# Half of one token group's first layer as seven products of halves, in an attention + squared-ReLU kernel on one core

## The chip, the core and the metric

One of the eight cores of a Trainium2 chip runs the whole kernel. The metric is the time of one execution on the device, in microseconds (us). The engines named below are PE (TensorE, the matrix multiplier; PEld is its weight load), DVE (VectorE), ACT (ScalarE), POOL (GpSimd) and SP (SyncE, which here only issues DMAs).

## What is computed

```
scores = q @ k^T / 8 + bias            # 8 batches, 8 heads, 576 tokens, head size 64
x      = softmax(scores) @ v           # heads put side by side: x is 4608 x 512
h      = max(x @ w_in, 0)              # layer 1: w_in is 512 x 2048
out    = (h * h) @ w_out               # layer 2: w_out is 2048 x 512, out is 4608 x 512
```

Inputs and output are float32. Inside, matrices are float16 and sums float32.

## The kernel before

**Two parts.** Attention goes over 32 pairs of heads (`pair(p)`, four for each batch). The two layers go over NG = 9 groups of GT = 512 tokens (`layers(g)`, L1084). A batch has 576 tokens, so group 7 (tokens 3584 to 4095) and group 8 (4096 to 4607) both need rows of the last batch, and their layer 1 comes after the last pair.

**Attention of a pair.** PE makes scores into the two tiles `st` of PSUM (ring `r_set`, two banks each, L702), ACT turns them into exponentials in one of three slots of `pt` (ring `r_pt`, L713), DVE multiplies the bias in (L794), PE multiplies with v into the single bank `pv` (ring `r_pv`, L830 and L837), and DVE normalises the sums into `x` (L854, L859). From batch 2 on a DMA transpose issued by SP puts x, turned, into `xt` (L875); group 8 needs the last two of these.

**Layer 1 of a group** (L1102): 16 blocks of 128 columns of h. A block is four matmuls of 512 tokens, one for each 128 rows of w_in, into one of three banks `f` (ring `r_g`). ACT takes the ReLU of the bank into one of four tiles `rt` (L1123), which frees the bank, and DVE squares it into `g` (L1133).

**Layer 2 of a group** is already done by seven products of halves in place of eight, in Winograd's form (`second(g)`, L980). DVE makes sums and differences of quarters of g (`sums_of_activations`, L958, rows with L972), the seven products (1 2 6 5 7 3 4) are run in two halves each, eight matmuls of 256 columns at a time (L1017): 14 steps. Each product is read out of its bank by ACT (L1051) or by DVE, which adds an earlier result held in a float32 tile `y` (L1045). SP stores finished quarters (L1073).

**What sets the order.** Nothing is issued in the order of the source. Every step is an `Op` with the engines that can do it, a modelled cost, what it depends on, the buffers that it holds, and a due time. `Plan.schedule` (L109) plays these through once: at each turn it takes the operation that can start first, and among those that can start at the same time the one with the smallest due time. What comes out is the fixed order of the instructions on each engine. A free engine never waits for an operation of earlier due time that isn't ready, and a started one isn't broken off. `one_of` (L284) marks an operation that either of two engines may do. The due time of group g is 60000 + 39000 g; its layer 1 blocks are due 2000 apart from there, and the 14 steps of layer 2 of the group before stand between them, 1000 behind the blocks, in the last group a further LATE2 = 7000 later (L1142).

**Buffers.** PSUM has eight banks: two tiles `st` of two banks, one bank `pv`, three banks `f`. After the last pair `st` and `pv` have no work from attention; in layer 2 of group 8 `pv` holds product 2. In the same way `stg` (staged q and k), the slots of `pt` and the float32 tiles `f32` (staged v) have no work left after the last pairs.

The calls that make a block of layer 1:

```
for i in range(16):
    if i < len(atoms1):
        nt, f1, bank = atoms1[i]
        o = P.add({"PE": 4 * mm(512)}, f1, xt_ready[g] + [l_win[nt // 4]], [bank, gb1], due + i * 2000, 0.0, "f")
```

Of the kernel before, what the change touches and what calls it, by code (L numbers as in the profile page):

```python
# [11 lines left out]
FP16 = mybir.dt.float16  # L12
EXPF = mybir.ActivationFunctionType.Exp
RELUF = mybir.ActivationFunctionType.Relu
COPYF = mybir.ActivationFunctionType.Copy
MULT = mybir.AluOpType.mult

# [8 lines left out]
GT = 512  # L26
# [13 lines left out]
SIX = 2  # L40
V_EARLY, V_HW = 18900.0, 2
LATE2 = 7000
T_POOL, T_DUE = 0, 0
ORDER = "k0 i0 q1 q0 v i1 o0 k1 i2 o1 o2 i3 o3"
HALF = GT // 2
# [135 lines left out]
def mm(n):  # L181
    return n / 2.4 + 2.5
# [6 lines left out]
def dve(n, rate=1.0, fix=160.0):  # L189
    return fix + n / (0.96 * rate)  # L190
# [3 lines left out]
def kernel(  # L194
# [13 lines left out]
    def io(ins):  # L208
        tc.keep_in_program_order(ins)
        return ins  # L210
# [399 lines left out]

    xt_ready, x_last = {}, {}
    x_bufs = {}

    def copy_to(engs_n, out_f, in_f, deps, bufs, due, fp16=True, dve_only=False):

# [13 lines left out]
    def pair(p):  # L629
# [63 lines left out]
        def run(jts):  # L693
            sets = [Buf(r_set) for _ in jts]

            def score():
                kt, qt = kts[qb.slot], qts[qb.slot]
                for jt, st in zip(jts, sets):
                    for e in range(2):
                        rw = ds(64 * e, 64)  # L700
                        io(
                            nc.tensor.matmul(  # L702
                                sets_ps[st.slot][:, e, :], kt[rw, ts(jt, 128)], qt[rw, 0:512],
                                start=True, stop=True,
                            )
                        )

            o = P.add({"PE": len(jts) * mm(512) + 10}, score, evac, sets + [qb, pb], T, after, "r")
            for jt, st in zip(jts, sets):

                def ex(jt=jt, st=st):
                    io(
                        nc.scalar.activation(  # L713
                            out=p5(pts[pb.slot])[:, jt, :, 0:512], in_=sets_ps[st.slot], func=EXPF, scale=SCALE
                        )
                    )

                exps[jt] = P.add({"ACT": act(1024)}, ex, [o], [st, pb], T)
# [214 lines left out]
    def sums_of_weights():  # L933
# [21 lines left out]
            done.append(o)  # L955
        return done

    def sums_of_activations(g):  # L958

        gb = g_bufs[g]  # L960
        sb_ = s_bufs[g] = {i: Buf(r_s[i]) for i in (1, 2, 4)}
        for c0 in (0, 4):
            o = None
            for to, uses in ((1, [1]), (2, [1, 2]), (4, [2, 4]), (3, [])):

                def add(to=to, c0=c0):
                    a11, a12, a21, a22 = (fourth(gb, eo, t, c0, 4) for t in range(2) for eo in range(2))
                    s = {i: ss[i][:, c0 : c0 + 4] for i in (1, 2, 4)}
                    out_, a, b_ = {
                        1: (s[1], a21, a22), 2: (s[2], a11, s[1]), 4: (s[4], a12, s[2]), 3: (a21, a21, a11)  # L970
                    }[to]
                    io(nc.vector.tensor_tensor(out=out_, in0=a, in1=b_, op=mybir.AluOpType.subtract))  # L972

                o = P.add(
                    {"DVE": dve(1024, 2.0)}, add, squares[g][2 * c0 : 2 * c0 + 8] + [o],
                    [gb] + [sb_[i] for i in uses], G0 + GP * g - 5e4,
                )
                s_done.setdefault((g, to), []).append(o)

    def second(g):  # L980
# [25 lines left out]
        for i in (int(x) for x in (P_LAST if g == NG - 1 else P_ORDER).split()):  # L1006
            bk, left, right, ns = prod[i]
            own = bk == "e" and g == NG - 1
            home = pv_ps if own else g_ps
            apart = bk == "d" and g == NG - 1  # L1010
            for s_ in range(2):
                bf = bank[f"d{s_}" if bk == "d" else bk]

                def mul(i=i, s_=s_, bf=bf, left=left, right=right, apart=apart, own=own, home=home):
                    for c in range(8):
                        io(
                            nc.tensor.matmul(  # L1017
                                home[bf.slot][:, ts(s_, HALF)], left(c, s_), right(c),
                                start=(c == 0 and (s_ == 0 or apart) and (own or i not in before)), stop=(c == 7),
                                skip_group_check=True,  # L1020
                            )
                        )

                def atom(d, i=i, s_=s_, bf=bf, ns=ns, mul=mul, own=own):
                    deps = d + [x for n in ns for x in s_done[g, n]] + squares[g]
                    deps += read_of[before[i]] if i in before and not own else []
                    deps += l_wout if i in (1, 2) else t_done
                    return P.add(
                        {"PE": 8 * mm(HALF)}, mul, deps, [bf, gb] + [sb_[n] for n in ns if n != 3], 1e6, 0.0, "f",
                    )  # L1030

                atoms.append(atom)
                if s_ == 0 and not apart:
                    continue

                def fin(o, i=i, bf=bf, s0=s_ if apart else 0, n=1 if apart else 2, own=own, home=home):
                    to, plus, where = reads[i]
                    plus = "u" if own else plus
                    cs = ds(s0 * HALF, n * HALF)

                    def ev():
                        dst, ps = ys[y[to].slot][:, cs], home[bf.slot][:, cs]
                        if plus is not None:
                            io(
                                nc.vector.scalar_tensor_tensor(  # L1045
                                    out=dst, in0=ps, scalar=OSC, in1=ys[y[plus].slot][:, cs], op0=MULT,
                                    op1=mybir.AluOpType.add,
                                )
                            )
# [30 lines left out]

                atoms.append(fin)
        return atoms

    def layers(g):  # L1084

        due = G0 + GP * g
# [2 lines left out]
        if g < NG:  # L1089
            g_bufs[g] = Buf(r_gb)  # L1090
            gb1 = g_bufs[g]
            squares[g] = []
            for nt in range(16):
                bank = Buf(r_g)

                def f1(nt=nt, bank=bank):
# [10 lines left out]
                            )  # L1107

                atoms1.append((nt, f1, bank))
        i2 = 0  # L1110
        last = None
        for i in range(16):
            if i < len(atoms1):
                nt, f1, bank = atoms1[i]
                o = P.add(
                    {"PE": 4 * mm(512)}, f1, xt_ready[g] + [l_win[nt // 4]], [bank, gb1], due + i * 2000, 0.0, "f"
                )
                f1_last[g] = o
                rb = Buf(r_rt)
# [1 line left out]
                def relu(o, bank=bank, rb=rb):  # L1121
# [4 lines left out]

                engs = {"ACT": act(512), "DVE": dve(512)} if g < RELU_DVE else {"ACT": act(512)}
                r = one_of(engs, relu, [o], [bank, rb], 0.0)
                squares[g].append(
                    P.add(  # L1130
                        {"DVE": dve(512, 2.0)},
                        lambda rb=rb, nt=nt, gb1=gb1: io(
# [64 lines left out]
```

## Time and profile before

| | |
|---|---|
| median of 5 runs | 373.41 us (372.42 to 374.81) |
| the profiled execution: its own time | 372.33 us |
| the profiled execution: its span | 370.5 us |
| granted clock of PE, mean | 0.999 |
| last matmul of layer 2 of group 7, end | about 355.2 us after the span's start |
| last matmul of the kernel, end | about 367.4 us |

The span is what the rows of the trace cover; 1.8 us of the execution lie around it. A row of a group gives the line, the engine, the operation, the tile written and the tiles read, the shapes and the count; behind the bar the busy time and the mean of one, and behind the second bar the idle time of the engine ahead of these instructions and what ended it. Matmuls overlap in their records (a record of 380 ns follows the one before it by 216 ns), so their cost is read from the chain of waits, which gives each piece the time by which it moves the end on.

### The profile page before, as it was taken

Reading aid. Unit: us, or ns where it says so; the run is one execution under the profiler, and the core shown is the slowest. Engines: PE = TensorE matmul, PEld = TensorE weight load, DVE = VectorE, ACT = ScalarE, POOL = GpSimd, SP = SyncE. Lnnn points to the kernel's source line nnn. Section 1 sums busy time; section 2 is a strip of 40 time slices with the busy share of each in tenths; the row PEclk is TensorE's granted clock in tenths of the full one; section 3 lists DMA queues with packets and bytes.
Section 4 is the critical chain, followed back from the end, with each engine's and each line's share of the span. In section 5 each row is a group of like instructions: output and inputs, shape, how many; then the busy total and the mean of one; then the engine's idle time right before and its main releaser. Section 6 shows DMA issues by size and latency. Waiting matters only on the chain.

```text
span 370.5 us, 9910 instructions
## 1 busy us (share of the span) xinstructions
PE 355.0 (96%) x3930; PEld 242.4 (65%) x3930; DVE 265.3 (72%) x594; ACT 257.5 (69%) x367; POOL 185.9 (50%) x343
## 2 busy tenths in 40 slices
PE   3978999899999999999999999999999999999996
PEld 2656455556587457877785468645877688546785
DVE  3997789967775598668865787579765985583573
ACT  4998989688576887679766887688659870564220
POOL 8897359394655686666855548667623000000000
PEclk9999999999999999999999999999999999999999
DMA  9999999795999999997999799999965113100022
GB/s 177 151 134 171 187 174 92 99 114 97 176 129 126 163 148 114 142 181 138 120 137 147 115 145 135 130 174 151 114 106 132 46 42 79 58 2 28 30 85 87
DMA packets 162293, 44.25 MB, mean 119 GB/s; under 512 B 145735, under 2 KB 162247, under 8 KB 162247
## 3 DMA queue, kind: packets, MB, share of 16 engines
q0 software_dynamic: 74208, 14.53, 49.9%
q1 hardware_dynamic: 87696, 28.80, 41.0%
q8 instruction: 31, 0.51, 0.6%
q10 hardware_dynamic: 342, 0.30, 0.3%
q14 instruction: 16, 0.12, 0.1%
HBM read 36.88 MB, written 9.44 MB: 125 GB/s over the span
## 4 chain that ended last, share of the span: by engine, by line
PE 88%; DVE 7%; ACT 2%; DMA 1%; issue 1%; ACTq 0%; DVEq 0%
PE f L1102 34%; PE f L1017 29%; PE pv L837 9%; PE st L702 8%; PE pv L830 2%; DVE pt L794 2%; PE st L751 2%; PE st L726 1%; DVE x L859 1%; DMA g<-in_q_dram 1%; PE f L657 1%; ACT pm L761 1%; DVE s L972 1%; DVE kt L621 1%; PE f L359 1%
## 5 line engine op out<-in xcount | busy, mean ns | idle before, releaser
L713 ACT ACTIVATE pt<-st 128x1024 f16<-128x1024 f32 x128 | 127.4, 1026 | 30.8 <-PE st L702 30.8
L1102 PE MATMUL f<-xt,w_in_sb 128*128 128x512 f16 (+4 forms) x704 | 138.5, 341 | 0.2 <-ACT xt L619 0.2
L1123 ACT ACTIVATE rt<-f 128x512 f16<-128x512 f32 x144 | 85.2, 602 | 49.2 <-PE f L1102 44.9
L1102 PEld LDWEIGHTS <-w_in_sb 128*128 128x128 f16 x704 | 62.6, 98 | 57.3 <-issue 12.2
L1133 DVE TENSOR_TENSOR g<-rt 128x512 f16<-128x512 f16 x144 | 64.3, 451 | 36.0 <-ACT rt L1123 35.2
L794 DVE TENSOR_TENSOR pt<-pt,tb_sb 128x1536 f16<-128x1536 f16 (+2 forms) x96 | 60.7, 640 | 15.1 <-ACT pt L713 14.4
L1017 PEld LDWEIGHTS <-g 128*128 128x128 f16 x576 | 54.5, 98 | 14.5 <-issue 4.7
L276 POOL DMA_DIRECT2D qs<-in_q_dram x79 | 55.4, 715 | 4.5 <-DMA w_out_sb<-in_moe_w_out_dram 2.7
L276 POOL DMA_DIRECT2D ks<-in_k_dram x79 | 55.3, 703 | 1.2 <-issue 1.2
L837 PE MATMUL pv<-va,pt 128*128 128x65 f16 x1280 | 54.7, 193 | 0.0
L837 PEld LDWEIGHTS <-pt 128*128 128x128 f16 x1280 | 50.2, 97 | 3.2 <-issue 1.4
L1045 DVE SCALAR_TENSOR_TENSOR y<-f,y 128x512 f32<-128x512 f32 (+1 forms) x47 | 31.4, 668 | 23.0 <-PE f L1017 22.7
L1017 PEld LDWEIGHTS <-s 128*128 128x128 f16 x432 | 41.2, 98 | 9.8 <-issue 2.5
L702 PE MATMUL st<-qt,kt 64*128 64x512 f16 x256 | 40.4, 386 | 0.9 <-ACT pt L736 0.4
L684 POOL COPY qz<-kt 64x64 f16<-64x64 f16 x58 | 19.7, 339 | 38.3 <-DMA kt<-ks 29.6
L684 POOL COPY qz<-qt 64x64 f16<-64x64 f16 x61 | 18.6, 305 | 37.8 <-DMA qt<-qs 17.0
L830 PE MATMUL pv<-vm,pm 128*128 128x130 f16 x160 | 35.3, 221 | 1.2 <-DVE x L859 1.0
L1017 PE MATMUL f<-wt,g 128*128 128x256 f16 x288 | 36.2, 273 | 0.0
L1017 PE MATMUL f<-w_out_sb,s 128*128 128x256 f16 x288 | 36.1, 273 | 0.0
L1017 PE MATMUL f<-w_out_sb,g 128*128 128x256 f16 x272 | 34.5, 273 | 0.7 <-ACT y L1051 0.7
L859 DVE TENSOR_TENSOR x<-pv,r 128x384 f16<-128x384 f32 x64 | 31.4, 491 | 2.0
L972 DVE TENSOR_TENSOR s<-g,s 128x1024 f16<-128x1024 f16 x36 | 25.7, 714 | 0.4
(66 smaller groups left out, 283.8 us busy)
## 6 DMA issues: line engine op xcount, KB each, us to landing
out_dram<-y SPq DMA_DIRECT2D x34, 256.0 KB, 2.3
f<-in_v_dram SPq DMA_DIRECT2D x24, 256.0 KB, 4.1
qs<-in_q_dram POOLq DMA_DIRECT2D x48, 64.0 KB, 4.0
ks<-in_k_dram POOLq DMA_DIRECT2D x48, 64.0 KB, 3.7
w_in_sb<-in_moe_w_in_dram POOLq DMA_DIRECT2D x4, 512.0 KB, 7.3
w_out_sb<-in_moe_w_out_dram POOLq DMA_DIRECT2D x4, 512.0 KB, 10.3
qs<-in_q_dram POOLq DMA_DIRECT2D x7, 144.0 KB, 4.4
ks<-in_k_dram POOLq DMA_DIRECT2D x7, 144.0 KB, 5.6
```

The costliest lines, as they stand in the source:

```text
L276: lambda: io(eng.dma_start(out=out_(), in_=in_())),
L684: io(eng.tensor_copy(out=dst[qb.slot][rw, rw], in_=src[qb.slot][rw, 512:576]))
L702: nc.tensor.matmul(sets_ps[st.slot][:, e, :], kt[rw, ts(jt, 128)], qt[rw, 0:512], start=True, stop=True,)
L713: nc.scalar.activation(out=p5(pts[pb.slot])[:, jt, :, 0:512], in_=sets_ps[st.slot], func=EXPF, scale=SCALE)
L794: io(nc.vector.tensor_tensor(out=a, in0=a, in1=t, op=MULT))
L830: nc.tensor.matmul(ps[:, i, :, :], pm[:, c : c + 128], vm[:, hp, :, 0:65], start=True, stop=False)
L837: nc.tensor.matmul(ps[:, i, e, :], pt[:, (2 * jt + e) * S + c : (2 * jt + e) * S + c + 128], va[:, jt, 2 * hp + e, 0:65], start=False, sto ...
L859: nc.vector.tensor_tensor(out=xs[xb.slot][:, qt0 : qt0 + nq, :].rearrange("p t (e d) -> p t e d", e=2), in0=ps[:, :, :, 0:64], in1=rs[rb.s ...
L1017: nc.tensor.matmul(home[bf.slot][:, ts(s_, HALF)], left(c, s_), right(c), start=(c == 0 and (s_ == 0 or apart) and (own or i not in before ...
L1102: nc.tensor.matmul(g_ps[bank.slot][:, a:z], w_in_sb[:, kk, ts(nt, 128)], xt_sb[:, kk, c : c + z - a], start=(kk == 0), stop=(kk == 3),)
L1123: io(nc.scalar.activation(out=rts[rb.slot], in_=g_ps[bank.slot], func=RELUF))
L1133: nc.vector.tensor_tensor(out=gs[gb1.slot][:, nt, :], in0=rts[rb.slot], in1=rts[rb.slot], op=MULT)
```

## The change

Only group 8, the last, is touched (`UNITS = {8: 2}`). Of its 16 blocks of layer 1, eight (nt 0 to 3 and 8 to 11) are replaced by two **units**. A unit takes 256 + 256 columns of h (the same place in both halves of w_in's 2048 columns), all 512 tokens in two halves of 256, and the 512 rows of w_in in two halves: a product of matrices of 2 by 2 parts. It is done by Winograd's seven products in place of eight.

- **Sums of x** (`t_ops`): four DVE instructions of 128x512 float16 on `xt`, into the tiles `stg` of the first two slots, once for the group. They depend on all of the group's `xt`; their due time is 100000 ahead of the group's, so DVE takes them before most else.
- **Sums of w_in** (`late["ops", u]`): four DVE instructions of 128x512 float16 for each unit, into a slot of `pt` that is claimed like that of one more pair. They depend on the scores of the last pair having been issued; their due time is the group's, so DVE takes them when nothing else can start.
- **Products**: each is four matmuls of 256 tokens (two blocks of 128 columns by two times 128 rows). The seven use four banks: products 1 and 2 in a tile `st` ("a"), 6 in a bank `f` ("b"), 5 and 3 in `pv` ("c"), 7 and 4 in the other tile `st` ("d"). 2, 3 and 4 are added onto what 1, 5 and 7 left in the bank, and so have to wait until that has been read (`after_read`).
- **Reads**: ACT copies 1 to a float32 tile u; DVE adds u to 6 (into u); ACT takes the ReLU of the bank with 1 + 2 straight into a tile `rt`; DVE adds u to 5 (into v, a tile `y` of layer 2's ring), v to 7, u to 3 and u to 4, the last three into tiles `rt`, of which ACT then takes the ReLU in place. Each of the four results of 128x512 is squared by DVE or by ACT (`SQUAREF`), whichever the plan finds free first.
- **Due times**: the products of a unit are due at (8u + AT) * 2000, AT = 0, 0.5, 2, 2.5, 4, 5.5, 7; the eight blocks that stay at (2d + 1) * 2000; the steps of layer 2 of group 7 where they were.
- `squares[g]` is now kept by block, so that the sums of activations of group 8 wait for the units' squares too: a half of them needs results of both units.

```
UNITS = {8: 2}
AT = (0, 0.5, 2, 2.5, 4, 5.5, 7)
...
        t_ops = late_sums(
            512, t,
            [
                (1, (lambda: xq(0, 1), lambda: xq(0, 0), SUB)),
                (2, (lambda: xq(1, 1), lambda: t(1), SUB)),
                (4, (lambda: xq(1, 0), lambda: t(2), SUB)),
                (3, (lambda: xq(1, 1), lambda: xq(0, 1), SUB)),
            ],
            xt_ready[g], due - 1e5,
        )
...
                late["ops", u] = late_sums(
                    512, s_,
...
                    l_win + last_scores, due + 10.0 * u, [late["room"]],
                )
            banks = {"a": Buf(r_set), "b": Buf(r_g), "c": Buf(r_pv), "d": Buf(r_set)}
            y = {"u": Buf(r_f), "v": Buf(r_y)}
            prod = {
                1: ("a", lambda u=u: wq(0, 0, u), lambda: xq(0, 0), True),
                6: ("b", lambda s_=s_: s_(2), lambda: t(2), True),
                2: ("a", lambda u=u: wq(0, 1, u), lambda: xq(1, 0), False),
                5: ("c", lambda s_=s_: s_(1), lambda: t(1), True),
                7: ("d", lambda s_=s_: s_(3), lambda: t(3), True),
                3: ("c", lambda s_=s_: s_(4), lambda: xq(1, 1), False),
                4: ("d", lambda u=u: wq(1, 1, u), lambda: t(4), False),
            }
            reads = {
                1: ("u", None, None), 6: ("u", "u", None), 2: (None, None, (0, 0)), 5: ("v", "u", None),
                7: (None, "v", (1, 1)), 3: (None, "u", (0, 1)), 4: (None, "u", (1, 0)),
            }
            after_read = {2: 1, 3: 5, 4: 7}
            for n, i in enumerate((1, 6, 2, 5, 7, 3, 4)):
...
                def mul(left=left, right=right, first_=first_, ps=ps):
                    for f in range(2):
                        for kk in range(2):
                            io(
                                nc.tensor.matmul(
                                    ps()[:, ts(f, HALF)], left()[:, kk, ts(f, 128)], right()[:, kk, :],
                                    start=(first_ and f == 0 and kk == 0), stop=(kk == 1), skip_group_check=True,
                                )
                            )
                o = P.add(
                    {"PE": 4 * mm(HALF)}, mul,
                    xt_ready[g] + t_ops + late["ops", u] + (read_of[after_read[i]] if i in after_read else []),
                    [st, gb1, late["room"]], due + (8 * u + AT[n]) * 2000.0, 0.0, "f",
                )
...
                e = one_of({"DVE": dve(512) + 100.0} if plus else {"ACT": act(512) + 100.0}, ev, deps, bufs, 0.0)
...
                e = one_of({"DVE": dve(512, 2.0), "ACT": act(512)}, square, [e], [rb, gb1], due - 1e5)
```

More of the change, by code (lines that the diff above doesn't have):

```diff
@@ L14 @@
 RELUF = mybir.ActivationFunctionType.Relu
+SQUAREF = mybir.ActivationFunctionType.Square
 COPYF = mybir.ActivationFunctionType.Copy
@@ L612 @@
     x_bufs = {}
+    last_scores = []
     def copy_to(engs_n, out_f, in_f, deps, bufs, due, fp16=True, dve_only=False):
@@ L708, in run @@
             o = P.add({"PE": len(jts) * mm(512) + 10}, score, evac, sets + [qb, pb], T, after, "r")
+            if p == 4 * B - 1:
+                last_scores.append(o)
             for jt, st in zip(jts, sets):
@@ L956, in sums_of_weights, with made @@
         return done
+    def made(g, a, z):
+        return [x for nt in range(a, z) for x in squares[g][nt]]
     def sums_of_activations(g):
@@ L974, in sums_of_activations @@
                 o = P.add(
-                    {"DVE": dve(1024, 2.0)}, add, squares[g][2 * c0 : 2 * c0 + 8] + [o],
+                    {"DVE": dve(1024, 2.0)}, add, made(g, 2 * c0, 2 * c0 + 8) + [o],
                     [gb] + [sb_[i] for i in uses], G0 + GP * g - 5e4,
@@ L1024, in atom @@
                 def atom(d, i=i, s_=s_, bf=bf, ns=ns, mul=mul, own=own):
-                    deps = d + [x for n in ns for x in s_done[g, n]] + squares[g]
+                    deps = d + [x for n in ns for x in s_done[g, n]] + made(g, 0, 16)
                     deps += read_of[before[i]] if i in before and not own else []
@@ L1082, in second, with sum_of_w, late_sums @@
         return atoms
+    late = {}
+    def sum_of_w(i, u):
+        return pts[late["room"].slot][:, ts(i - 1, 1024)].rearrange("p (k c) -> p k c", k=2)[:, :, ts(u, 256)]
+    def late_sums(n, dst, terms, deps, due, bufs=()):
+        o, made_ = None, []
+        for i, (a, b_, op) in terms:
+            o = P.add(
+                {"DVE": dve(n, 2.0)},
+                lambda i=i, a=a, b_=b_, op=op: io(nc.vector.tensor_tensor(out=dst(i), in0=a(), in1=b_(), op=op)),
+                deps + [o], bufs, due,
+            )
+            made_.append(o)
+        return made_
@@ new lines, with by_sevens, ev, square @@
+    SUB = mybir.AluOpType.subtract
+    def by_sevens(g, units, due):
+        assert max(UNITS.values()) <= 2
+        if not late:
+            late["room"] = Buf(r_pt)
+        c = (g * GT) % XR
+        assert c + GT <= XR
+        wq = lambda i, k, u: w_in_sb[:, 2 * k : 2 * k + 2, 1024 * i + 256 * u : 1024 * i + 256 * u + 256]
+        xq = lambda k, j: xt_sb[:, 2 * k : 2 * k + 2, c + HALF * j : c + HALF * j + HALF]
+        o_ = 4 * (g - min(UNITS)) - 1
+        t = lambda i: stg[(i + o_) // 2][(i + o_) % 2][:, 0:512].rearrange("p (k c) -> p k c", k=2)
+        t_ops = late_sums(
+            512, t,
+            [
+                (1, (lambda: xq(0, 1), lambda: xq(0, 0), SUB)),
[4 more added lines that the diff above has]
+            xt_ready[g], due - 1e5,
+        )
+        gb1 = g_bufs[g]
+        for u in range(units):
+            s_ = lambda i, u=u: sum_of_w(i, u)
+            if ("ops", u) not in late:
+                late["ops", u] = late_sums(
+                    512, s_,
+                    [
+                        (1, (lambda u=u: wq(1, 0, u), lambda u=u: wq(1, 1, u), mybir.AluOpType.add)),
+                        (2, (lambda s_=s_: s_(1), lambda u=u: wq(0, 0, u), SUB)),
+                        (4, (lambda u=u: wq(0, 1, u), lambda s_=s_: s_(2), SUB)),
+                        (3, (lambda u=u: wq(0, 0, u), lambda u=u: wq(1, 0, u), SUB)),
+                    ],
+                    l_win + last_scores, due + 10.0 * u, [late["room"]],
+                )
+            banks = {"a": Buf(r_set), "b": Buf(r_g), "c": Buf(r_pv), "d": Buf(r_set)}
+            y = {"u": Buf(r_f), "v": Buf(r_y)}
+            at = lambda i, y=y: (fs if i == "u" else ys)[y[i].slot]
+            prod = {
+                1: ("a", lambda u=u: wq(0, 0, u), lambda: xq(0, 0), True),
[5 more added lines that the diff above has]
+                4: ("d", lambda u=u: wq(1, 1, u), lambda: t(4), False),
+            }
+            reads = {
+                1: ("u", None, None), 6: ("u", "u", None), 2: (None, None, (0, 0)), 5: ("v", "u", None),
+                7: (None, "v", (1, 1)), 3: (None, "u", (0, 1)), 4: (None, "u", (1, 0)),
+            }
+            after_read = {2: 1, 3: 5, 4: 7}
+            read_of = {}
+            for n, i in enumerate((1, 6, 2, 5, 7, 3, 4)):
+                bk, left, right, first_ = prod[i]
+                st = banks[bk]
+                if bk in "ad":
+                    ps = lambda st=st: sets_ps[st.slot][:, 0, :]
+                else:
+                    ps = lambda st=st, home=g_ps if bk == "b" else pv_ps: home[st.slot]
+                def mul(left=left, right=right, first_=first_, ps=ps):
+                    for f in range(2):
+                        for kk in range(2):
+                            io(
+                                nc.tensor.matmul(
+                                    ps()[:, ts(f, HALF)], left()[:, kk, ts(f, 128)], right()[:, kk, :],
+                                    start=(first_ and f == 0 and kk == 0), stop=(kk == 1), skip_group_check=True,
+                                )
+                            )
+                o = f1_last[g] = P.add(
+                    {"PE": 4 * mm(HALF)}, mul,
+                    xt_ready[g] + t_ops + late["ops", u] + (read_of[after_read[i]] if i in after_read else []),
+                    [st, gb1, late["room"]], due + (8 * u + AT[n]) * 2000.0, 0.0, "f",
+                )
+                to, plus, where = reads[i]
+                deps = [o]
+                if plus == "u":
+                    deps += read_of[1 if i == 6 else 6]
+                if plus == "v":
+                    deps += read_of[5]
+                bufs = [st] + [y[x] for x in {to, plus} - {None}]
+                rb = Buf(r_rt) if where else None
+                bufs += [rb] if rb else []
+                def ev(e, to=to, plus=plus, ps=ps, at=at, rb=rb):
+                    dst = rts[rb.slot] if rb else at(to)
+                    if plus is not None:
+                        io(
+                            nc.vector.scalar_tensor_tensor(
+                                out=dst, in0=ps(), scalar=1.0, in1=at(plus), op0=MULT, op1=mybir.AluOpType.add
+                            )
+                        )
+                    else:
+                        io(nc.scalar.activation(out=dst, in_=ps(), func=RELUF if rb else COPYF))
+                e = one_of({"DVE": dve(512) + 100.0} if plus else {"ACT": act(512) + 100.0}, ev, deps, bufs, 0.0)
+                read_of[i] = [e]
+                if not rb:
+                    continue
+                if plus is not None:
+                    e = P.add(
+                        {"ACT": act(512)},
+                        lambda rb=rb: io(nc.scalar.activation(out=rts[rb.slot], in_=rts[rb.slot], func=RELUF)),
+                        [e], [rb], 0.0,
+                    )
+                def square(o, rb=rb, where=where, u=u):
+                    src = rts[rb.slot].rearrange("p (f s) -> p f s", f=2)
+                    n0 = 8 * where[0] + 2 * u
+                    dst = gs[gb1.slot][:, n0 : n0 + 2, ts(where[1], HALF)]
+                    if o.eng == "ACT":
+                        io(nc.scalar.activation(out=dst, in_=src, func=SQUAREF))
+                    else:
+                        io(nc.vector.tensor_tensor(out=dst, in0=src, in1=src, op=MULT))
+                e = one_of({"DVE": dve(512, 2.0), "ACT": act(512)}, square, [e], [rb, gb1], due - 1e5)
+                for f in range(2):
+                    squares[g][8 * where[0] + 2 * u + f].append(e)
@@ L1091, in layers @@
             gb1 = g_bufs[g]
-            squares[g] = []
-            for nt in range(16):
+            squares[g] = {nt: [] for nt in range(16)}
+            units = UNITS.get(g, 0)
+            for nt in [nt for nt in range(16) if nt % 8 >= 2 * units]:
                 bank = Buf(r_g)
@@ L1109, in layers, with place @@
                 atoms1.append((nt, f1, bank))
+            if units:
+                by_sevens(g, units, due)
+            def place(d):
+                return 2 * d + 1 if d < 4 * units else 4 * units + d
         i2 = 0
         last = None
+        skip = 16 - len(atoms1) if g < NG else 0
         for i in range(16):
-            if i < len(atoms1):
-                nt, f1, bank = atoms1[i]
+            if i >= skip and g < NG:
+                nt, f1, bank = atoms1[i - skip]
                 o = P.add(
-                    {"PE": 4 * mm(512)}, f1, xt_ready[g] + [l_win[nt // 4]], [bank, gb1], due + i * 2000, 0.0, "f"
+                    {"PE": 4 * mm(512)}, f1, xt_ready[g] + [l_win[nt // 4]], [bank, gb1], due + place(i - skip) * 2000,
+                    0.0, "f",
                 )
@@ L1128, in layers @@
                 r = one_of(engs, relu, [o], [bank, rb], 0.0)
-                squares[g].append(
+                squares[g][nt].append(
                     P.add(
```

## The prediction

> **What bounds the kernel now.** The change lies behind the last pair, so I read the end of the span, first the chain of waits from 317 us on (start, time by which the piece moves the end on, what, how many instructions):
>
> ```profile
> 317.90 14.68 PE f L1102 x68
> 332.57 0.87 PE f L1017 x8
> 333.45 0.86 PE f L1102 x4
> ...
> 352.56 1.73 PE f L1102 x8
> 354.29 2.62 PE f L1017 x24
> 356.91 1.75 PE pv L1017 x16
> 358.65 8.75 PE f L1017 x80
> 367.40 0.02 issue
> 367.43 0.42 DVE y L1045
> ```
>
> Every piece is PE's and each starts where the last one ends. Two prices follow. A matmul of 512 columns moves the end by 14.68/68 = 0.216 us, so a block of layer 1 costs 0.864. One of 256 columns costs 8.75/80 = 0.109, so a step of layer 2 (eight) costs 0.875. The 68 are 17 blocks; with three before them, 20 blocks were done at 332.57, 16 of group 7 and four of group 8: group 8 begins at 332.57 - 4 x 0.864 = 329.1. Now the busy time by stretch (columns: sum, then PE, PEld, DVE, ACT, POOL with counts, clock, DMA share, GB/s): the last pair, layer 1 of group 7, layer 1 of group 8 with layer 2 of group 7, and layer 2 of group 8.
>
> ```profile
> 301.50:313.56 12.06, 12.06 (x177) 11.09 (x176) 7.00 (x15) 2.97 (x4) 0.00 (x0) 1.00 0.23 52
> 313.56:329.10 15.54, 15.54 (x82) 7.84 (x80) 9.56 (x21) 8.96 (x15) 0.00 (x0) 1.00 0.17 55
> 329.10:355.16 26.06, 26.06 (x179) 17.27 (x177) 14.38 (x30) 11.34 (x19) 0.00 (x0) 1.00 0.09 31
> 355.16:367.43 12.27, 12.23 (x113) 10.71 (x110) 7.45 (x14) 0.60 (x1) 0.00 (x0) 1.00 0.21 68
> ```
>
> PE has no gap in any of them, at full clock. Third stretch by work: 16 blocks x 0.864 + 14 steps x 0.875 = 13.82 + 12.25 = 26.07, which is the stretch. DVE is idle for 11.7 us of it and ACT for 14.7. So here PE's work alone sets the end: what leaves PE is gained, and what makes PE wait is lost, one for one. Last, the rows that price the new work of DVE and ACT, from the groups by line between 329.1 and 355.2 us and, for the table load, of the whole run:
>
> ```profile
> L1133 DVE TENSOR_TENSOR g<-rt 128x512 f16<-128x512 f16 x18 | 7.6, 424 | 11.3 <-ACT rt L1123 11.2
> L1045 DVE SCALAR_TENSOR_TENSOR y<-f,y 128x512 f32<-128x512 f32 x4 | 2.8, 688 | 0.8 <-PE f L1017 0.7
> L1123 ACT ACTIVATE rt<-f 128x512 f16<-128x512 f32 x17 | 10.1, 597 | 13.3 <-PE f L1102 12.1 <-DVE g L972 1.1
> L317 ACT ACT_TABLE_LOAD x1 | 1.3, 1283 | 2.7 <-issue 2.7
> ```
>
> **What leaves and what comes on PE.** Out: eight blocks, 32 matmuls x 0.216 = 6.91 us. In: 2 units x 7 products x 4 = 56 matmuls of 256 columns x 0.109 = 6.12 us. Sum: -0.79 us. No other PE work changes. The new matmuls have the shape of layer 2's, a weight load of 98 ns (its row) under each 109 ns, so that price carries over.
>
> A rule of the Trainium skill speaks against this step. The page "TensorE: Matmul & The Clock Gate", section "Back-to-back issue gap", gives the spacing of weight load and matmul pairs in a real stream as about 131 ns at 512 columns and 81 at 128. On a straight line between them 256 columns cost about 98 (an estimate from that page); 32 x 131 = 4.2 us would leave and 56 x 98 = 5.5 come, and the kernel would lose 1.3 us. The trace contradicts it: 216 and 109 in this kernel, the shorter one at very nearly half. I take the rows: -0.79.
>
> **What comes on DVE and ACT in the third stretch.** Each unit adds five reads with an addition on DVE (688 ns, L1045's kind): 10 x 0.69 = 6.9 us. Eight squares of blocks go, eight squares of units come (0.42 each on DVE, or 0.60 on ACT). ACT loses eight ReLUs and gets two units x (copy of 1, ReLU of 1+2, three ReLUs in place) = 10, +1.2 us; if it gets all squares, +4.8 more. DVE stands between 17.9 (squares on ACT) and 21.3 (on DVE) of 25.3 us, ACT between 12.5 and 17.3. Both fit, DVE at 71 to 84%. So no engine replaces PE on average; what counts is whether single waits reach PE.
>
> **The new waits, in the order that the due times give.** With P for a product, R for a block, S for a step: P1 P6 R P2 P5 R S P7 S R P3 S S P4 R, then P1 S P6 S R P2 S P5 S R P7 S S R P3 S P4 S R S S. P2, P3 and P4 stop PE's queue until P1, P5, P7 have been read, and all matmuls behind them wait too. Nearest cover is P1 to P2: one product and one block between, 0.44 + 0.86 = 1.30 us; an ACT read begins 0.04 us after its block (a block ends at 334.31, its ReLU begins at 334.35) and runs 0.60. Between P5 and P3, and P7 and P4, lie at least 2.1 us, for one DVE read of about 0.8. Each of the six waits may cost between nothing and one DVE instruction that stands ahead of the read, 0.69 us (4.1 in all), less than nothing in no case, since there is no gap to close. I take nothing, as L1017's own P2, P3 and P4, which wait in the same manner in this stretch, show no gap. Banks: b is held by P6 until DVE has read it, while layer 2 holds up to two of the three banks f; blocks then share one, as now (blocks 2.6 us apart from 346.5 us on, without a gap).
>
> At the end of the stretch two steps (1.75 us) stand behind the last block in place of one; now its ReLU and square are done 1.09 us after it (block's end 354.29, square's end 355.38). The sums of g then come later than now, since both halves need the last unit: products 1 and 2 of group 8 (3.5 us) cover four of them (start to start 0.6 to 0.7 each, 2.7 us) before product 6 needs them. Covered by about 2 us; without the cover, up to 2.7.
>
> **Sums of x.** Four on DVE, 0.42 each by L1133, 1.7 us. They wait for the last transposes, whose DMAs land 2.3 to 3.8 us after the last issue at 313.4. If they stand too early in DVE's queue, the squares of group 7 wait behind them, then the tiles rt, then ACT, then PE. Four rt and three banks hold several blocks at 0.86 us, so a DVE stop of up to about 3 us shows nothing, and DVE has 6 us idle in that stretch to catch up. At most 1 us beyond, from a landing at 317.2 with DVE at it from 313.4; I take nought.
>
> **Sums of w_in.** Eight x 0.42 = 3.4 us, from about 301.5 on, when the last scores are out and the slot of pt of pair 29 is free. DVE is idle 5.06 of the 12.06 us there, in gaps of 0.2 to 1.1. Sums that straddle the end of a gap put off a normalisation (four are left), each by less than 0.42, and behind a normalisation wait the single bank pv and, through SP's transposes, layer 1 of group 7. PE has steps of layer 2 of group 6 to fill with: two still stand between blocks at 314.4 and 317.0 (1.75 us). Between 0 and 3.4 us; I take 0, because the sums yield to whatever else can start.
>
> **Square on ACT.** The trace of before has one table load, 1.28 us, and no Square. If Square needs another table, one load falls into ACT's idle 14.7 us: ReLUs late by 1.3 us, of which the spare banks hide most. "ScalarE: Activation LUTs", section "Table sets: the hidden batching unit", says that cheap functions, of which it names relu, copy, identity and abs, are in every set, and puts a switch at about 2.7 us with the drain. By the row 1.3, by the page 2.7; in either case I take nothing on PE.
>
> **The sum.** 372.33 of the profiled execution (span 370.5 and 1.8 around it) - 0.79 = 371.5. The median of the runs is 1.1 above that execution; the same step gives 373.41 - 0.8 = 372.6.
>
> **Rivals.**
> - **The gain is eaten by small waits of PE** (a read that comes late, the single bank f, a sum ahead of a normalisation). For it: DVE rises from 55% to 71 or 84%, and its 0.69 us instructions can't be broken off. Against it: today's plan holds PE without a gap for 54 us. One or two waits of 0.4 to 0.7 us: 372.9 to 374.0, say 373.4.
> - **Sums of w_in on the path of the last pair: slower.** All eight stand ahead of normalisations and nothing fills PE: 3.4 - 0.8 = +2.6, 376.0. It beats the gain from the second sum on (2 x 0.42), and is slower by over 0.5% from the seventh (1.87 + 0.79 = 2.7 us of waiting). For it: recip and norm follow their matmuls within 0.2 us. Against it: 5.06 us of gaps for 3.4 us of work.
> - **Faster by more than the arithmetic.** PE has no wait in these stretches that could go, so only the scatter of runs could show it.
>
> **Chances.** Full gain 0.60 (372.6; own range 372.1 to 373.0), eaten 0.22, slower by the sums of w_in or by a longer queue on DVE 0.14, faster 0.04. Half a per cent, 1.87 us, is about what a measurement of this kernel can tell from no change: faster 0.04, same 0.82, slower 0.14. The range 371.9 to 374.2 takes the first two cases and their scatter and leaves out the slower one.
>
> **What would show it.** Right: the last matmul ends near 366.6 us; 32 matmuls of blocks and 56 new ones in a third stretch of about 25.3 us, without idle time of PE; new reads at 0.69 us. Wrong: idle PE ahead of a product with ACT or DVE named (first rival), or ahead of the first block at 313.6 (second); the sums of w_in at more than 0.42; a second table load; the new matmuls spaced by more than 109 ns.

## The result and the profile after

The changed kernel takes 372.59 us in the median of 44 runs (371.23 to 374.57) against 373.18 of the kernel before (79 runs taken beside it). The ratio is 0.9981, with a 95% interval from 0.9972 to 0.9989: faster by 0.19%, 0.7 us, with 0.4 to 1.0 inside the interval. The forecast was -0.8 us and a time of 372.6. That the time agrees to the hundredth is luck: the kernel before measured 0.23 us less than the 373.41 that the forecast started from, and the two medians differ by 0.59 and not by 0.8. The gain is real and far below the half per cent that the prediction took as its bound for a difference.

The scatter of single runs (over 3 us) is larger than the effect, so the trace is the better ruler if it is measured between two points of PE. I take the start of the 16 matmuls of layer 2 that follow the last pair's last scores (301.51 us in the profile before, 301.26 after) and the end of the last matmul (367.40 and 366.36). Between them lie 65.89 us before and 65.10 after: **-0.79 us**. The other 0.25 us by which the last matmul comes earlier arose ahead of anything that the change touches. Below, "the end stretch" is this distance. The pieces with which it starts, before and after:

```profile
301.51 1.85 PE f L1017 x16
301.26 1.85 PE f L1028 x16
```

The chain of waits after (start, time by which the piece moves the end on, what, how many instructions; L1257 are the blocks of layer 1, L1182 the new products, L1028 the steps of layer 2):

```profile
312.98 2.08 PE f L1028 x19
315.06 13.81 PE f L1257 x64
328.87 0.44 PE st L1182 x4
329.31 0.44 PE f L1182 x4
329.75 0.86 PE f L1257 x4
330.61 0.44 PE st L1182 x4
331.05 0.44 PE pv L1182 x4
...
351.51 0.86 PE f L1257 x4
352.37 3.49 PE f L1028 x32
355.87 1.75 PE pv L1028 x16
357.61 8.75 PE f L1028 x80
366.36 0.02 issue
366.38 0.42 DVE y L1056
```

It is still PE without a break. A product of four matmuls moves the end by 0.44 us, 0.109 each, which is the price that was taken from layer 2. The busy time of the same four stretches (last pair, group 7, group 8 with the units, layer 2 of group 8; columns as before):

```profile
301.25:315.06 13.81, 13.81 (x193) 12.65 (x192) 9.99 (x24) 2.97 (x4) 0.00 (x0) 1.00 0.26 66
315.06:328.87 13.81, 13.81 (x66) 6.32 (x65) 10.33 (x24) 8.96 (x15) 0.00 (x0) 1.00 0.13 41
328.87:354.12 25.25, 25.25 (x203) 19.57 (x201) 18.10 (x33) 16.02 (x27) 0.00 (x0) 1.00 0.10 32
354.12:366.38 12.26, 12.22 (x112) 10.71 (x110) 8.16 (x14) 0.60 (x1) 0.00 (x0) 1.00 0.21 69
```

The third stretch is 25.25 us long in place of 26.06, DVE has gone from 14.38 to 18.10 in it and ACT from 11.34 to 16.02. The new work, from the groups by line (of five like rows of DVE reads one is shown):

```profile
L1230 ACT ACTIVATE g<-rt 128x512 f16<-128x512 f16 x8 | 5.0, 630 | 0.3
L1221 ACT ACTIVATE rt<-rt 128x512 f16<-128x512 f16 x6 | 3.8, 630 | 2.3 <-DVE rt L1207 2.3
L1108 DVE TENSOR_TENSOR pt<-w_in_sb 128x512 f16<-128x512 f16 x4 | 1.6, 418 | 0.0
L1207 DVE SCALAR_TENSOR_TENSOR rt<-st,y 128x512 f16<-128x512 f32 x2 | 1.4, 692 | 0.6 <-PE st L1182 0.6
L321 ACT ACT_TABLE_LOAD x1 | 1.3, 1283 | 2.6 <-issue 2.6
```

Reads take 692 ns, sums 418, all eight squares ran on ACT (L1230) at 630, and Square needed no second table load.

### The profile page after: what moved, and what is told of

It is laid out like the page before. It is cut to its first block, busy times and chain, and to the rows that moved or that the text cites. A ratio compares the mean times of both kernels' runs of the same rounds, so it can differ in the third digit from the quotient of the medians.

```text
span 369.4 us, 9991 instructions
## 1 busy us (share of the span) xinstructions
PE 354.3 (96%) x3954; PEld 244.6 (66%) x3954; DVE 273.4 (74%) x610; ACT 262.2 (71%) x375; POOL 188.6 (51%) x343
## 4 chain that ended last, share of the span: by engine, by line
PE 88%; DVE 7%; ACT 2%; DMA 1%; issue 1%; ACTq 0%; DVEq 0%
PE f L1257 33%; PE f L1028 29%; PE pv L844 9%; PE st L707 8%; PE pv L837 2%; PE st L758 2%; DVE pt L801 2%; PE st L733 1%; DVE x L866 1%; DMA g<-in_q_dram 1%; PE st L1182 1%; PE f L662 1%; ACT pm L768 1%; DVE s L983 1%; PE f L363 1%
## 5 line engine op out<-in xcount | busy, mean ns | idle before, releaser
L1257 PE MATMUL f<-xt,w_in_sb 128*128 128x512 f16 (+4 forms) x672 | 130.9, 339 | 0.2 <-ACT xt L624 0.2
L1286 ACT ACTIVATE rt<-f 128x512 f16<-128x512 f32 x136 | 80.4, 602 | 41.7 <-PE f L1257 37.7
L1257 PEld LDWEIGHTS <-w_in_sb 128*128 128x128 f16 x672 | 59.4, 98 | 54.4 <-issue 12.7
L1296 DVE TENSOR_TENSOR g<-rt 128x512 f16<-128x512 f16 x136 | 59.9, 445 | 24.4 <-ACT rt L1286 23.3
L1028 PEld LDWEIGHTS <-g 128*128 128x128 f16 x576 | 54.5, 98 | 13.0 <-issue 4.7
L1028 PEld LDWEIGHTS <-s 128*128 128x128 f16 x432 | 41.2, 98 | 8.7 <-issue 2.5
L689 POOL COPY qz<-qt 64x64 f16<-64x64 f16 x61 | 20.0, 328 | 32.1 <-DMA qt<-qs 24.9
L1028 PE MATMUL f<-w_out_sb,s 128*128 128x256 f16 x288 | 36.1, 273 | 0.0
L1028 PE MATMUL f<-wt,g 128*128 128x256 f16 x288 | 35.7, 273 | 0.0
L1028 PE MATMUL f<-w_out_sb,g 128*128 128x256 f16 x272 | 34.5, 273 | 0.7 <-ACT y L1062 0.7
```

The lines of the kernel that those rows point to most:

```text
L689: io(eng.tensor_copy(out=dst[qb.slot][rw, rw], in_=src[qb.slot][rw, 512:576]))
L1028: nc.tensor.matmul(home[bf.slot][:, ts(s_, HALF)], left(c, s_), right(c), start=(c == 0 and (s_ == 0 or apart) and (own or i not in before ...
L1257: nc.tensor.matmul(g_ps[bank.slot][:, a:z], w_in_sb[:, kk, ts(nt, 128)], xt_sb[:, kk, c : c + z - a], start=(kk == 0), stop=(kk == 3),)
L1286: io(nc.scalar.activation(out=rts[rb.slot], in_=g_ps[bank.slot], func=RELUF))
L1296: nc.vector.tensor_tensor(out=gs[gb1.slot][:, nt, :], in0=rts[rb.slot], in1=rts[rb.slot], op=MULT)
```

## The experiments

**Theory**: in the end stretch only PE's work counts, as long as every wait of PE is covered; the change takes 0.79 us of that work away and all its waits are covered. **Rivals**: the gain comes from another order of the end, whatever the amount of PE work; small waits already eat part of it, so that more work on DVE or ACT would show at once; the sums of w_in lie on the path. In all ten kernels the whole of the computation is done. The end stretch is measured from the same two points in each, in one trace of each kernel.

| kernel | ratio to before (95%) | end stretch, us | against before | PE idle in it, us |
|---|---|---|---|---|
| before | | 65.89 | | none |
| the change | 0.9981 (0.9972 to 0.9989) | 65.10 | -0.79 | none |
| one unit | 0.9994 (0.9980 to 1.0007) | 65.49 | -0.40 | none |
| three units | 0.9974 (0.9960 to 0.9987) | 64.70 | -1.19 | none |
| four units | 1.0101 (1.0062 to 1.0139) | 68.91 | +3.02 | 2.4 |
| two units in groups 7 and 8 | 1.0018 (1.0004 to 1.0033) | 66.45 | +0.56 | 1.8 |
| the same, results in tiles of their own | 1.0042 (1.0012 to 1.0071) | 68.42 | +2.53 | 2.1 |
| before, eight blocks in halves | 0.9992 (0.9978 to 1.0005) | 65.98 | +0.09 | none |
| squares on DVE | 0.9972 (0.9957 to 0.9986) | 65.10 | -0.79 | none |
| banks from one ring | 1.0012 (0.9997 to 1.0028) | 66.01 | +0.12 | 0.5 |
| sums of w_in first | 1.0021 (1.0007 to 1.0034) | 66.40 | +0.51 | 1.0 |
| reads doubled | 1.0025 (1.0012 to 1.0038) | 67.03 | +1.14 | 1.8 |

Idle is the time that the trace puts down as waiting; each gap costs some 0.16 us more, since the first matmul behind it doesn't overlap with the one before (a record of 273 ns at a spacing of 109 ns: a first product of 0.60 us in place of 0.44). The two longest end stretches, +3.02 and +2.53, hold another 1.7 us each in which the granted clock was below 1; the last section comes to that.

**One unit, and three.**

```
-UNITS = {8: 2}
+UNITS = {8: 1}
```

> One unit in place of two (UNITS = {8: 1}), so four blocks of layer 1 are replaced and not eight. If the gain is PE's work alone, 16 matmuls x 0.216 leave and 28 x 0.109 come, -0.40 us against the kernel before, ratio 0.9989, and the last matmul ends 0.4 us after that of the changed kernel, with PE still without a gap. If the gain came from another order of the end (a fixed effect of any unit), it stays at 0.7 to 0.8 us.

The end stretch is shorter by 0.40, as PE's work says; a fixed effect of the order is excluded by the trace. The ratio alone couldn't tell it from no change. For three units I also moved due times, and gave the third unit's sums a second slot of pt:

```
-LATE2 = 7000
-UNITS = {8: 2}
-
-AT = (0, 0.5, 2, 2.5, 4, 5.5, 7)
+LATE2 = 20000
+UNITS = {8: 3}
+
+AT = (0, 0.5, 1, 1.5, 2, 2.5, 3)
...
-                    l_win + last_scores, due + 10.0 * u, [late["room"]],
+                    l_win + last_scores, due + 10.0 * u, [late["room", u // 2]],
```

> Three units in group 8 (UNITS = {8: 3}, the sums of the third in a second slot of pt), with the steps of layer 2 of group 7 due later (LATE2 = 20000) and the products of a unit due closer together (AT = 0, 0.5, 1, 1.5, 2, 2.5, 3). By PE's work 3 x 0.395 = -1.18 us against the kernel before (ratio 0.9968) if no wait reaches PE: DVE gets 5 more reads, 3.5 us, ACT two more operations of each kind. If DVE's and ACT's chains are already at their limit, as in the kernel with units in two groups, gaps show and the gain falls below that of two units, 0.79.

Measured -1.19 us in the end stretch, without a gap, in the stretch of the products that is now 24.85 us long:

```profile
330.47:355.32 24.85, 24.85 (x215) 20.76 (x213) 20.18 (x35) 17.80 (x31) 0.00 (x0) 1.00 0.07 24
```

DVE is at 81% there and ACT at 72%. This version beats both kernels: by 0.40 us more than the change in the end stretch, while the intervals of the two ratios overlap. One, two and three units give -0.40, -0.79 and -1.19: a straight line. Three units with the first due times were not tried.

**Eight blocks in halves of 256 columns**, the price of a matmul by itself, on the kernel before:

```
...
+                    if g == NG - 1 and nt % 8 < 4:
+                        n = HALF
-                    for a, z, c in ((0, n, c), (n, GT, 0)):
+                    for a, z, c in ((0, n, c), (n, GT, c + n if n == HALF else 0)):
```

> The kernel before, with the same eight blocks of group 8 run as matmuls of 256 columns in place of 512 (64 in place of 32, the same work, no products of seven). By the rows of the trace (0.109 and 0.216) it costs 64 x 0.1094 - 32 x 0.2159 = +0.09 us, not to be told from no change. By the spacing that the skill's page gives (98 estimated at 256 columns, 131 at 512) it costs 64 x 0.098 - 32 x 0.131 = +2.1 us, ratio 1.006.

Measured +0.09 us in the end stretch. Eight matmuls of 256 columns move the end by 0.87 us in the trace, where four of 512 move it by 0.86:

```profile
341.68 0.87 PE f L1104 x8
```

The row's price holds to the hundredth; the page's spacing, with which the halves would cost an estimated 2.1 us, isn't this kernel's.

**Squares on DVE.**

```
-e = one_of({"DVE": dve(512, 2.0), "ACT": act(512)}, square, [e], [rb, gb1], due - 1e5)
+e = one_of({"DVE": dve(512, 2.0)}, square, [e], [rb, gb1], due - 1e5)
```

> The changed kernel with all eight squares of the units on DVE (in the changed kernel all eight ran on ACT, 0.63 each). DVE then has 18.1 + 8 x 0.42 = 21.5 us of 25.25. If single waits reach PE at such a load (the first rival), idle PE of 0.4 us and more shows and the gain shrinks; if there is slack, the time is that of the changed kernel within 0.1 us (ratio 0.998 to the kernel before).

The end stretch is 65.10, that of the change. The busy time in the stretch of the products:

```profile
330.91:356.16 25.25, 25.25 (x203) 19.57 (x201) 19.52 (x38) 12.07 (x21) 0.00 (x0) 1.00 0.10 32
```

The load was less than I expected, 19.5 us of DVE (77%) and not 21.5. DVE has five instructions more than in the change, not eight: the eight squares came, but two reads of layer 2 went back from DVE to ACT (L1062) and one sum of g fell behind the end of the stretch. So the run tries less than I meant it to, but it shows that at the change's load, 18.1 us, there is room to spare.

**Banks from one ring.**

```
-banks = {"a": Buf(r_set), "b": Buf(r_g), "c": Buf(r_pv), "d": Buf(r_set)}
+banks = {i: Buf(r_g) for i in "abcd"}
...
```

> The changed kernel with the units' four banks all taken from the ring of three banks f, in place of one f, the bank pv and the two tiles st. If the four separate tiles are what keeps the single waits away from PE, gaps of PE show in the stretch of group 8's layer 1, since a unit then holds up to two of three banks (c from product 5 to the read of 3, d from 7 to the read of 4) while layer 2 of group 7 holds one or two: two to five waits of about half a microsecond, 1 to 2.5 us, so slower than the kernel before by 0.2 to 1.7 us. If banks are not scarce, the time is that of the changed kernel.

Two waits, of about a quarter of a microsecond each and not of half: 0.91 us lost against the change, just under the 1 to 2.5 that I expected, so all of its gain and 0.12 more. This is one of them; the product behind the block (L1179) waits until the ReLU of that block (L1283) has freed its bank; one other product, not in the chain, runs in between:

```profile
333.03 0.88 PE f L1254 x4
333.91 0.02 issue
333.93 0.61 ACT rt L1283
334.54 0.04 issue
334.58 0.60 PE f L1179 x4
```

So the banks outside the ring ("a", "c" and "d") are worth 0.91 us here: without them the change gains nothing.

**Sums of w_in first.**

```
-l_win + last_scores, due + 10.0 * u, [late["room"]],
+l_win + last_scores, -1e6 + 10.0 * u, [late["room"]],
```

> The changed kernel with the due time of the eight sums of w_in set ahead of everything, so that DVE takes all eight as soon as the last scores are out, before the last pair's products with the bias and its normalisations (3.4 us). The prediction's slower rival says that nothing fills PE: 3.4 us of idle PE ahead of the first block of group 7, +2.6 us against the kernel before. My theory: PE has layer 2 of group 6 to fill with, of which two steps (1.75 us) stood between blocks in the kernel before; so idle PE is at most 3.4 - 1.75 = 1.65 us, and the time is at most 0.9 us above the kernel before.

It loses 1.30 us against the change and is 0.51 slower than before: within my bound and far from the rival's +2.6. The chain runs through DVE, which comes to the last products with the bias and to a normalisation late, and PE's pv waits for that:

```profile
309.44 0.02 issue
309.46 0.69 DVE y L1056
310.15 0.11 DVE pt L801
310.26 0.21 issue
310.46 0.19 DVE r L861
310.65 0.02 issue
310.68 0.43 DVE x L866
311.11 0.04 issue
```

Of 3.4 us of sums, 1.3 reach PE. The rival's mechanism exists; it is the due time that keeps it away.

**Reads doubled.**

```
+                        io(
+                            nc.vector.scalar_tensor_tensor(
+                                out=stg[4][1][:, 0:512], in0=ps(), scalar=1.0, in1=at(plus), op0=MULT,
+                                op1=mybir.AluOpType.add,
+                            )
+                        )
...
-                e = one_of({"DVE": dve(512) + 100.0} if plus else {"ACT": act(512) + 100.0}, ev, deps, bufs, 0.0)
+                e = one_of({"DVE": 2 * dve(512) + 100.0} if plus else {"ACT": act(512) + 100.0}, ev, deps, bufs, 0.0)
```

> The changed kernel with each of the ten DVE reads of the units done twice (the first into a spare tile), ten more instructions of 0.69 us. DVE then has 18.1 + 6.9 = 25.0 us of the stretch's 25.25. If DVE's load is what decides, this is the point at which it becomes the bound: PE shows gaps of 2 to 5 us in all, at the products that wait for a read and at the first product of group 8's layer 2 that waits for sums of g. If slack on DVE doesn't matter (another thing bounds the end), the time stays that of the changed kernel.

One gap of 1.8 us, a little under what I expected and at neither of the places that I named: it lies in product 7 of group 7's layer 2, whose second four matmuls wait for the last sum of g of that group. DVE makes this sum at 350.5 us here, and made it at 337.8 in the change: its backlog has put it off. The end stretch is 1.93 longer than the change's. DVE is busy 23.9 of 26.0 us. The end of the chain through DVE, and the wait:

```profile
349.67 0.60 DVE rt L1213
350.27 0.33 DVE g L1302
350.61 0.61 DVE g L983
351.22 0.05 issue
351.26 6.72 PE f L1028 x60
```

**Two units in groups 7 and 8; then their results in tiles of their own.**

```
-UNITS = {8: 2}
+UNITS = {7: 2, 8: 2}
```

> Two units in group 7 as well (UNITS = {7: 2, 8: 2}); group 7's layer 1 also lies behind the last pair. By PE's work: -0.79 us twice, 1.58 against the kernel before, ratio 0.9958, if DVE keeps up: in the stretch of group 7's layer 1 (13.8 us, DVE 10.3 busy) it gets some 7 us more of reads and loses squares to ACT. The rival, waits for DVE: that stretch would fill (17 of 13.8 us less what moves), PE shows gaps ahead of the products or of the blocks and the second 0.79 is lost or turned into a loss.

With 1.58 us less work of PE the end stretch grew by 0.56, so waits cost 2.14. Two gaps: 1.23 us ahead of a block, and 0.58 in product 6 of group 7's layer 2, which waited for a sum of g; with 0.16 more for each they make 2.13. The first, in ACT's instructions (start, duration, line, tiles, idle time ahead):

```profile
326.96 0.62 ACT L1221 ACTIVATE rt<-rt 128x512 f16<-128x512 f16 x1
328.18 1.23 ACT L1221 ACTIVATE rt<-rt 128x512 f16<-128x512 f16 x2 [0.59 <-DVE rt L1207]
329.31 2.29 ACT L1286 ACTIVATE rt<-f 128x512 f16<-128x512 f32 x4
```

Four blocks' ReLUs (L1286) stand behind in-place ReLUs of the units, which wait for reads by DVE; until they run, the three banks f are full. To see whether the four tiles rt, which both need, set that order, the units' results went to a slot of pt:

```
-rb = Buf(r_rt) if where else None
+rb = Buf(late["rt"]) if where else None
...
+at_rt = lambda rb=rb: pts[late["more"].slot][:, ts(rb.slot, 512)]
```

> The kernel with units in groups 7 and 8, with one thing changed: the units' results go through eight tiles of their own in a free slot of pt, and no longer through the ring of four tiles rt that the blocks' ReLUs use. If the first gap there (1.23 us before a block, which waited for a ReLU that stood in ACT's queue behind in-place ReLUs) came from the four rt, that gap goes. If the work of DVE and ACT as a whole is the limit, PE's idle time only moves to the end of the layer-1 stretch, to the steps of layer 2 that wait for sums of g, and the time stays above that of the kernel before (with units in both groups it was 0.56 us above by the trace).

The first gap is gone (PE is busy for 4.92 of the 4.97 us from 328.60 to 333.57), so the tiles rt did cause it. But a gap of 2.07 us comes in product 1 of group 8's layer 2. It waits for a square of a unit on ACT, and not for a sum of g; both ACT (2.90 of 3.04 us) and DVE (2.87) are full there. The trace is longer still, mostly by the clock: without the 1.7 us of the last section its end stretch is 66.7 us, about that with shared tiles, 66.45. So the tiles of their own moved the wait and gained nothing.

**Four units.** The kernel with three, with `UNITS = {8: 4}`.

> Four units in group 8, that is all of its layer 1 by seven products, otherwise as the kernel with three units. PE's work alone: 4 x 0.395 = -1.58 us against the kernel before. DVE: with three units it has some 20 us in the stretch; the fourth adds 3.5 us of reads and the stretch gets shorter by 0.4, about 24 of 24.5 us, the load at which the kernel with doubled reads had gaps of 1.9 us. My theory: gaps of 1 to 4 us, so 0 to 2.5 us slower than the kernel before. If only PE counts, ratio 0.9958.

Slower by 3.0 us in the end stretch, above my range: gaps of 0.5, 0.2 and 1.7 us, and 1.7 us more by a lower granted clock, which the last section shows. Without that it is slower by 1.3, inside the range.

## Why the prediction was right

- **PE's work.** -0.79 was the whole sum, and it is what the end stretch measured. The price of 0.109 for 256 columns held in the products (0.44 for four) and in the halved blocks.
- **The Trainium skill's spacing** ("TensorE: Matmul & The Clock Gate", section "Back-to-back issue gap"). Weighed against the row and set aside; the halved blocks show that the row was the right choice.
- **DVE and ACT on average.** DVE was set at 17.9 us with all squares on ACT, and is at 18.10; that this is so close is luck. Two reads of layer 2 that ACT had done went to DVE, 1.38 us that the sum did not have; one sum of g less in the stretch (0.68) and a larger overlap of the records (some 0.5) took nearly as much off. For the same two reads ACT, set at 17.3, is at 16.02.
- **The new waits.** Taken at nothing, and PE has no gap. P1 ends at 329.31, ACT reads its bank from 329.40 to 329.99 (the row below), and P2 begins at 330.61: of the 1.30 us of cover 0.68 are used. That nothing reaches PE depends on the banks outside the ring f, as the run with one ring shows.

```profile
329.40 0.59 ACT L1212 ACTIVATE f<-st 128x512 f32<-128x512 f32 x1
```

- **The end of the stretch.** The outcome was right, the size wrong. I counted four sums of g ahead of product 6 and about 2 us to spare. DVE does the four of one half first, so six stand ahead; the last of them, the first in this row, is done at about 357.05 for a product that begins at 357.61. The margin is 0.56 us:

```profile
355.62 0.69 DVE L983 TENSOR_TENSOR s<-g 128x1024 f16<-128x1024 f16 x1
356.34 1.42 DVE L983 TENSOR_TENSOR s<-g,s 128x1024 f16<-128x1024 f16 x2
```

- **Sums of x.** They ran from 317.80 to 320.80 between squares of group 7, stopped by nothing.
- **Sums of w_in.** Right at zero, but not for the reason that I gave, that they yield. With them in the plan normalisations come later: one of the last pair begins 8.27 us into the end stretch, in place of 7.36 (309.53 and 308.87 us in the two traces). What hid it was the filler that I named beside it: the two steps of group 6 that had stood between blocks of group 7 now run ahead of the first of them, which begins at 315.06 and not at 313.56, at no cost in work.
- **Square on ACT.** One table load before and one after.
- **The rivals.** Small waits that eat the gain: none here, but they come with one ring of banks, with doubled reads, with units in both groups and with four units. The slower rival: its mechanism was worth 1.30 us when it was forced, against the 3.4 that it assumed.

## What to carry to other kernels

Where an engine has no gap at all over the last stretch, price a change by that engine's work, from the spacing of its own rows, and then check only that each new wait is covered. The reserve runs out on the engines that pay: here three units gained in a straight line with DVE at 81% of the stretch of the products, and gaps stood in every kernel with DVE at 85% and above. The share alone doesn't decide: the change has none at 72%, and the kernel with one ring of banks has two at 73%. Results that share a small ring of buffers with other work hold that work up, before an engine is full.

## What was not expected of the hardware

A gap of PE can cost a second time. After the 2.07 us of waiting in the kernel with units in both groups and tiles of their own, the granted clock (third number from the right in these rows) was 0.60 and then 0.85:

```profile
346.20:349.24 3.04, 0.97 (x9) 0.63 (x8) 2.87 (x6) 2.90 (x5) 0.00 (x0) 1.00 0.00 0
349.24:352.00 2.76, 2.76 (x16) 2.09 (x17) 1.99 (x3) 0.60 (x1) 0.00 (x0) 0.60 0.00 0
352.00:356.00 4.00, 4.00 (x33) 3.35 (x32) 0.88 (x2) 0.00 (x0) 0.00 (x0) 0.85 0.00 0
```

That is 2.76 x 0.40 + 4.00 x 0.15 = 1.7 us more, nearly as much as the gap. With four units, where 2.4 us of waits fall into 5.3, the clock was 0.74 over the next 6.67 us, again 1.7 us. After the gaps of 1.23 and of 1.8 us (units in both groups, reads doubled) it stayed at 1.00.

The length of the gap doesn't decide it alone, though. A loss of 1.7 us lowers the mean clock of an execution of 375 us to 0.995. Of the ten executions of the kernel with tiles of its own, five have a mean of 0.990 to 0.995 (the traced one 0.994), but the other five have 1.000, which leaves no room for the loss. Those five have a median of 373.95 us, and the eight of the kernel before at 0.999 or 1.000, taken beside them, one of 373.23: slower by 0.7, as the end stretch is without the 1.7 (+0.8). And a loss of that size comes without such a gap. In the traces with squares on DVE and with banks from one ring the clock is 0.66 from 25 to 30 us (5 x 0.34 = 1.7), far ahead of the change; in those of the kernel before and of the change it is 1.00 there, though PE waits at times in all four. So one and the same kernel shows the loss in some executions and not in others, and what decides that stays open.
